# Two sequences by turns: the order of token groups in a fused linear-attention and two-layer feed-forward kernel

## The chip, the cores and the metric

The kernel runs on one core of one Trainium2 chip. The core has a tensor engine (PE, with its weight loads as PEld), a vector engine (DVE), a scalar engine (ACT), GpSimd (POOL), and a sync engine (SP) that here issues nearly all transfers. The metric is device time in microseconds (us) of one execution; lower is better. A difference of about 2% is what a measurement of this kernel can surely tell from no change.

## What is computed

A linear attention with a decay per head and dimension gives x; a sum of four experts, weighted per token, follows, and then a feed-forward layer with a sigmoid gate. Sizes: 2 sequences of 768 tokens, 8 heads of 48, so 1536 tokens of width 384; 4 experts of 1024 hidden units; a last layer of 2048.

```python
for t in range(S):                      # per sequence and head
    cur = einsum('bhd,bhe->bhde', u[None] * kt, vt)
    y[:, :, t] = einsum('bhd,bhde->bhe', rt, state + cur)
    state = w[None, :, :, None] * state + einsum('bhd,bhe->bhde', kt, vt)
...
p = domain_probs / (domain_probs.sum(-1, keepdims=True) + 1e-09)
for e in range(E):
    h = np.maximum(x @ w1[e], 0.0)
    out += p[:, e:e + 1] * (h @ w2[e])
...
h = x @ w_in
g = h * (1.0 / (1.0 + np.exp(-1.702 * h)))
return g @ w_out
```

## The kernel before

The attention works on 12 groups of 128 tokens, `G`; groups 0 to 5 are the first sequence, 6 to 11 the second. For each group (`attention`) r and k are scaled by powers of the decay (`rr` on DVE, `kk` on DVE for groups 0 and 1 and on POOL for the others, `kb` on ACT), PE forms the scores of the 8 heads in two halves (`sc`), DVE copies them under the causal mask into `at` (whose diagonal, r u k of a token itself, POOL has made from `ruk` and `ss`), and PE multiplies `at` with the values (`y`). A group that isn't the first of its sequence adds the product of `rr` with the state `sn` to `y`. The state of the next group comes from `kc` (k by a table `tab`, on POOL), the product `kv` (PE), its part within the heads `sn` (DVE), and the decayed state before, `tn` (POOL). `y` is split into two float32r parts, `xh` (ACT) and `xl` (DVE).

The feed-forward layers run in six blocks of eight chunks of 128 hidden units: four experts, and the last layer in two halves. A unit is one chunk with one tile of tokens, 256 tokens in block 0 and 512 in the others. Its weights are split into `wh` (ACT) and `wl` (DVE), its hidden values into `gh` (ACT) and `gl` (DVE); each product is three matmuls (high by high, low by high, high by low), nine for `up` and nine for `dn`. The first tile of block 0, tokens 0 to 255, needs groups 0 and 1 alone. The router weights `pb` of an expert, 1536 floats, are copied to all 128 partitions through a scratch `pscr` in HBM. At the end DVE adds two blocks (`final`, into `tp`) and SP stores `tp` to `out_t`.

Nothing is issued in the order of the code. A planner (`Plan`) takes every operation with its engine, an assumed cost, a due time and what it reads and writes, plays them through and writes out one order for each engine; an engine then executes its own list strictly in that order. Changed due times or dependences can so move any operation of the early part. Matmuls called `warm`, on data of no meaning, fill planned gaps of PE before the first unit. Near the start there is also a check of the range of the decays, `wr`, `mm` and `flag`: six small DVE instructions that nothing but the end of the program needs.

Of the kernel before, what the change touches and what calls it, by code (L numbers as in the profile page):

```python
# [18 lines left out]
P = 128  # L19
# [17 lines left out]
NB = 8                  # chunks on chip, split  # L37
# [9 lines left out]
class Plan:  # L47
    """Operations in an order that is right one after another, and the order in which they are issued.

    Each names the engine, what it takes of it, when it is wanted, what it reads, writes and which  # L50
    buffers it takes. An engine that is free takes, of the operations that could start, the one wanted
    first.
    """
# [70 lines left out]
# what a transfer or an operation adds before another engine can go on  # L124
# [15 lines left out]
def c_mm(m, n, wide=True):  # L140
    # a product in float32, or in two parts
    return 2 * max(m / 1200, n / 1200) if wide else max(m / 1200, n / 2400)


def narrowing(nc, hi, lo, a, m, r):
    """The steps from the two words of a float64 to the float32 nearest to it."""
    dve, pool = nc.vector, nc.gpsimd
    f = lambda t: t().bitcast(F32)
    return (
        lambda: dve.tensor_scalar(out=m(), in0=hi(), scalar1=0x7fffffff, scalar2=None, op0=ALU.bitwise_and),  # L150
        lambda: dve.tensor_scalar(out=f(m), in0=f(m), scalar1=HI_MIN, scalar2=2.0 ** 16, op0=ALU.max, op1=ALU.mult),  # L151
        lambda: dve.tensor_scalar(  # L152
            out=m(), in0=m(), scalar1=4, scalar2=1, op0=ALU.logical_shift_left, op1=ALU.logical_shift_right),
        lambda: dve.scalar_tensor_tensor(  # L154
            out=a(), in0=hi(), scalar=-0x80000000, in1=m(), op0=ALU.bitwise_and, op1=ALU.bitwise_or),
        lambda: dve.tensor_scalar(out=m(), in0=a(), scalar1=-0x800000, scalar2=None, op0=ALU.bitwise_and),  # L156
        lambda: dve.scalar_tensor_tensor(  # L157
            out=f(m), in0=lo().bitcast(U32), scalar=2.0 ** -52, in1=f(m), op0=ALU.mult, op1=ALU.mult),
        lambda: pool.tensor_tensor(out=r(), in0=f(a), in1=f(m), op=ALU.add),  # L159
    )  # L160


def times(a, n, m):
    # the columns of a, m times
    return a.rearrange("p (o i) -> p o i", o=1).to_broadcast([n, m, a.shape[-1]])
# [18 lines left out]
def general(ctx: ExitStack, tc: tile.TileContext, wv, cst, msk, pscr, rk, tok, wts, wts2, out):  # L184
    """The whole again, for any decay: no power of it is negative.

    Within a group, the second half of a block of tokens looks at its first half, for blocks of every size.
    """
# [152 lines left out]
def body(outer: ExitStack, tc: tile.TileContext, wv, cst, msk, dp, rk, tok, wts, wts2, out):  # L341
# [45 lines left out]
    def warm():  # L387
        # keeps the tensor engine's clock up while its operands are on their way
        if "warm" not in T:
            T["warm"] = ps_dn.tile([P, 512], F32, tag="dn0", name="warm")  # L390
        pe.matmul(T["warm"][:, :G], lhsT=acc[:, 0, :G], rhs=acc[:, 0, :G], start=True, stop=True)
# [10 lines left out]
    def load_group(g, dues):  # L402
        def one(i):
            if i == 0:
                T["rk", g] = rk_p.tile([PD, 2, NP, G], F32, tag="rk", name="rk")
                sp.dma_start(T["rk", g], rk[g])
            elif i == 1:
                T["tok", g] = rk_p.tile([P, 2, DM], F32, tag="tok", name="tok")
                sp.dma_start(T["tok", g], tok[g, :, 0:2])
            else:  # L410
                T["val", g] = rk_p.tile([P, 2, DM], F32, tag="val", name="val")
                sp.dma_start(T["val", g], tok[g, :, 2:4])
# [72 lines left out]
    def power_table():  # L485
        # kept finite where the general path takes over
# [14 lines left out]
    def tables(due):  # L501
        # for the state: w^(191-j) by token, w^128 within the blocks of the heads
        kt = ac_p.tile([PD, NP, G], F32, name="kt")
# [54 lines left out]
    def load_p(e, due):  # L558
        def fn():
            T["pb", e] = pb_p.tile([P, NT], F32, tag="pb", name="pb")  # L560
            sp.dma_start(
                T["pb", e], pscr[e].rearrange("p n -> (p n)").rearrange("(a n) -> a n", a=1).to_broadcast([P, NT]))
        add("dma", 2.2, due, fn, reads=["pscr"], writes=[("pb", e)], takes=[("pb", 1, ("pb", e))])

# [1 line left out]
    def attention(g, due):  # L566
        first, final = g % GPB == 0, g % GPB == GPB - 1
# [7 lines left out]
        # decayed r and k, by dimension  # L575
# [28 lines left out]
        # r u k of a token itself, on the diagonal  # L604
# [66 lines left out]
        # the state: the sum of k v, decayed  # L671
        if not final:
# [13 lines left out]
            def own_():  # L686
                new(("sn", g + 1), [PD, NP, PD])
                dve.tensor_tensor(out=T["sn", g + 1], in0=T[kv], in1=times(own, PD, NP), op=ALU.mult)
# [3 lines left out]
            add("dve", c_dve(DM), due["kv"] + 1, own_, reads=[kv, "cs1"], writes=[("sn", g + 1)],  # L692
                takes=[("sn", 2, ("sn", g + 1))])
            if not first:
                add("pool", c_pool(DM), due["kv"] + 2, lambda: pool.tensor_tensor(
                    out=T["sn", g + 1], in0=T["sn", g + 1], in1=T["tn", g], op=ALU.add),
                    reads=[("tn", g)], writes=[("sn", g + 1)])
            if g % GPB < GPB - 2:
                def decay():
                    new(("tn", g + 1), [PD, NP, PD], bufs=1)  # L700
                    pool.tensor_tensor(out=T["tn", g + 1], in0=T["sn", g + 1], in1=wg, op=ALU.mult)
                add("pool", c_pool(DM), due["kv"] + 6, decay, reads=[("sn", g + 1), "wg"], writes=[("tn", g + 1)],
                    takes=[("tn", 1, ("tn", g + 1))])
# [59 lines left out]
    def unit(i):  # L763
# [68 lines left out]
        for j in range(3):  # L832
            # the last of all goes out in two parts
# [10 lines left out]
    def end(blk, j, dn, t0, n, due, cols):  # L844
# [27 lines left out]
        if blk == 0:  # L872
            add("dve", c_dve(n), due, scaled, reads=[dn, ("pb", 0), "warm"], writes=AK)
# [11 lines left out]
        else:  # L885
# [4 lines left out]
            o = out[j * P:(j + 1) * P, t0 + cols.start:t0 + cols.stop]  # L890
            add("dma", n / 640, due, lambda: sp.dma_start(o, T[TP][:, cols]), reads=[part])

# [1 line left out]
    def dues(b, d, prep):  # L894
# [10 lines left out]
    tables(-925)  # L905
    attention(0, {"scale": -970, "bonus": -970, "sc": (-960, -950), "mask": (-959, -949), "kc": -890, "kv": -880,
                  "av": (-955, -945), "out": -940})
    attention(1, {"scale": -930, "bonus": -930, "sc": (-920, -910), "mask": (-919, -909), "kc": -700, "kv": -600,
                  "av": (-860, -850), "out": -840})
# [100 lines left out]
```

## Time and profile before

| what | value |
|---|---|
| median of 3 runs | 710.98 us |
| the three runs | 706.25, 710.98 and 2824.54 us |
| span of the profiled execution | 704.3 us |
| PE busy, share of the span | 96% |
| DVE, ACT and POOL busy | 53%, 28% and 24% |
| mean granted clock of PE | 0.997 of full |

The times list no separate own time of the profiled execution: beside its span of 704.3 us stands the fastest run, 706.25 us. Busy shares are averages over stages that have different limits; in the first 40 us PE waits for other engines, and between 410 and 530 us for DVE.

### The profile page before, as it was taken

What the parts mean: (1) busy time and instruction counts of PE and PEld (TensorE: products, weight loads), DVE (VectorE), ACT (ScalarE), POOL (GpSimd) and SP (SyncE); (2) the same over time, 40 slices, a digit from 0 to 9 for tenths busy, and PEclk for the clock granted to TensorE, in tenths of its full rate; (3) what the DMA queues carried; (4) which work ended last, traced back from release to release, by engine and by line L of the source; (5) the groups of instructions that cost most, each with busy time, mean ns of one, the idle gap of its engine ahead of it and who ended that gap; (6) DMA issues with size and microseconds to landing.
All of it is one profiled execution on the core that took longest, in us unless ns stands there. A gap on an engine that the chain in (4) does not pass through costs nothing.

```text
span 704.3 us, 8976 instructions
## 1 busy us (share of the span) xinstructions
PE 677.8 (96%) x3644; PEld 580.4 (82%) x3644; DVE 374.9 (53%) x559; ACT 194.7 (28%) x351; POOL 169.2 (24%) x139
## 2 busy tenths in 40 slices
PE   8799999999999999999999998899799999999996
PEld 7799999999988888888888766688478888888885
DVE  7895544543622134412136999859993345434333
ACT  3432222212421123211123112133323344432231
POOL 6999356500001020202020334133430000000000
PEclk9999999999999999999999999999999999999999
DMA  7985223100420002300003442402100000001011
GB/s 228 288 241 168 66 68 91 46 1 1 136 89 1 0 1 91 129 5 0 1 24 111 180 134 91 134 1 89 46 0 1 1 0 1 0 1 46 1 45 49
DMA packets 12546, 45.90 MB, mean 65 GB/s; under 512 B 2129, under 2 KB 2642, under 8 KB 12498
## 3 DMA queue, kind: packets, MB, share of 16 engines
q1 hardware_dynamic: 12498, 45.26, 19.9%
q8 instruction: 30, 0.49, 0.3%
q14 instruction: 18, 0.15, 0.1%
HBM read 42.87 MB, written 2.38 MB: 64 GB/s over the span
## 4 chain that ended last, share of the span: by engine, by line
PE 76%; DVE 17%; POOL 3%; issue 2%; DMA 1%; ACT 0%; SPq 0%; DVEq 0%; POOLq 0%
PE dn L829 34%; PE up L775 34%; PE sc L661 4%; PE y L714 3%; DVE m L150 2%; DVE a L154 2%; DVE m L151 2%; DVE gl L794 1%; DVE wl L479 1%; DVE m L152 1%; PE y L718 1%; DVE m L156 1%; DVE m L157 1%; DMA rk<-in_rk 1%; DVE tp L855 1%
## 5 line engine op out<-in xcount | busy, mean ns | idle before, releaser
L775 PE MATMUL up<-xh,wh 128*128 128x512 f32 (+1 forms) x504 | 185.6, 368 | 8.2 <-DVE gl L794 6.6
L829 PE MATMUL dn<-gh,wh 128*128 128x512 f32 (+1 forms) x512 | 182.9, 357 | 4.3 <-DVE tp L855 4.1
L829 PE MATMUL dn<-gl,wh 128*128 128x512 f32 (+1 forms) x512 | 182.6, 357 | 2.4 <-DVE gl L813 2.4
L829 PE MATMUL dn<-gh,wl 128*128 128x512 f32 (+1 forms) x512 | 182.2, 356 | 0.0
L775 PE MATMUL up<-xl,wh 128*128 128x512 f32 (+1 forms) x504 | 181.0, 359 | 0.5 <-DVE xl L738 0.5
L775 PE MATMUL up<-xh,wl 128*128 128x512 f32 (+1 forms) x504 | 180.8, 359 | 0.0
L794 DVE SCALAR_TENSOR_TENSOR gl<-up,gh 128x512 fp32r<-128x512 f32 (+1 forms) x120 | 69.7, 582 | 168.0 <-ACT gh L788 167.7
L788 ACT ACTIVATE gh<-up 128x512 fp32r<-128x512 f32 (+1 forms) x120 | 61.4, 512 | 306.1 <-PE up L775 305.9
L775 PEld LDWEIGHTS up<-xh,wh 128*128 128x128 f32 x504 | 95.1, 189 | 26.2 <-DVE gl L794 10.4
L829 PEld LDWEIGHTS dn<-gh,wh 128*128 128x128 f32 x512 | 96.6, 189 | 20.8 <-DVE tp L855 2.3
L829 PEld LDWEIGHTS dn<-gl,wh 128*128 128x128 f32 x512 | 96.7, 189 | 17.1 <-DVE gl L813 3.0
L829 PEld LDWEIGHTS dn<-gh,wl 128*128 128x128 f32 x512 | 96.6, 189 | 13.7
L775 PEld LDWEIGHTS up<-xh,wl 128*128 128x128 f32 x504 | 95.0, 188 | 14.2
L775 PEld LDWEIGHTS up<-xl,wh 128*128 128x128 f32 x504 | 95.1, 189 | 13.9 <-DVE xl L738 0.7
L858 POOL TENSOR_TENSOR acc<-acc,tp 128x512 f32<-128x512 f32 x27 | 37.8, 1409 | 219.1 <-DVE tp L855 218.7
L809 DVE TENSOR_TENSOR gf<-up,sg 128x512 f32<-128x512 f32 x48 | 33.1, 690 | 75.2 <-ACT sg L805 75.2
L159 POOL TENSOR_TENSOR r<-a,m 128x768 f32<-128x768 f32 x16 | 32.0, 2001 | 90.8 <-DVE m L157 85.5
L805 ACT ACTIVATE sg<-up 128x512 f32<-128x512 f32 x48 | 28.6, 596 | 82.4 <-PE up L775 82.0
L813 DVE TENSOR_TENSOR gl<-gf,gh 128x512 fp32r<-128x512 f32 x48 | 33.4, 696 | 22.6 <-ACT gh L788 21.7
L788 ACT ACTIVATE gh<-gf 128x512 fp32r<-128x512 f32 x48 | 30.4, 632 | 41.4 <-DVE gf L809 41.0
L479 DVE TENSOR_TENSOR wl<-w,wh 128x768 fp32r<-128x768 f32 x32 | 34.1, 1069 | 2.8 <-ACT wh L475 2.2
L714 PE MATMUL y<-at,val 128*96 128x128 f32 x192 | 29.5, 281 | 1.6 <-DVE at L664 1.6
(78 smaller groups left out, 544.9 us busy)
## 6 DMA issues: line engine op xcount, KB each, us to landing
w<-in_wts SPq DMA_DIRECT2D x32, 768.0 KB, 4.5
rk<-in_rk SPq DMA_DIRECT2D x12, 384.0 KB, 4.4
tok<-in_tok SPq DMA_DIRECT2D x12, 384.0 KB, 4.5
val<-in_tok SPq DMA_DIRECT2D x12, 384.0 KB, 3.7
pb<-pscr SPq DMA_DIRECT2D x4, 768.0 KB, 4.5
out_t<-tp SPq DMA_DIRECT2D x8, 256.0 KB, 2.0
out_t<-tp SPq DMA_DIRECT2D x2, 128.0 KB, 3.4
cs<-in_cst SPq DMA_DIRECT2D x1, 192.5 KB, 4.3
```

What stands on the lines that cost most here:

```text
L159: lambda: pool.tensor_tensor(out=r(), in0=f(a), in1=f(m), op=ALU.add),
L479: dve.tensor_tensor(out=T[L_], in0=src(), in1=T[H_].bitcast(F32), op=ALU.subtract)
L661: pe.matmul(sc[:, j, :], lhsT=a[:n, h // 2, :], rhs=T[RR][:n, h // 2, :], start=True, stop=True)
L714: pe.matmul(y[:, p, :], lhsT=v2[:, h].rearrange("p b d -> p (b d)"), rhs=T["at", g, half][:, h % NP, :], start=hh == 0, stop=first and hh ...
L775: pe.matmul(T[U][:, :n], lhsT=a[:, s], rhs=b, start=d + k == 0, stop=d + k == 4)
L788: act.activation(out=T[GH][:, :n], in_=T[src][:, :n], func=f)
L794: dve.scalar_tensor_tensor(out=T[GL][:, :n], in0=T[U][:, :n], scalar=0.0, in1=T[GH][:, :n].bitcast(F32), op0=ALU.max, op1=ALU.subtract)
L805: act.activation(out=T[SG][:, :n], in_=T[U][:, :n], func=ACTF.Sigmoid, scale=1.702)
L809: dve.tensor_tensor(out=T[GF][:, :n], in0=T[U][:, :n], in1=T[SG][:, :n], op=ALU.mult)
L813: dve.tensor_tensor(out=T[GL][:, :n], in0=T[GF][:, :n], in1=T[GH][:, :n].bitcast(F32), op=ALU.subtract)
L829: pe.matmul(T[dn][:, cols], lhsT=T[a][:, s], rhs=T[b][:, cols], start=first and k == 0, stop=last and k == 2)
L858: pool.tensor_tensor(out=av, in0=av, in1=T[TP][:, :n], op=ALU.add)
```

## The change

The groups of the two sequences are taken by turns: with `ORDER`, place q of the plan holds group q // 2 of sequence q % 2. Places 0 and 1 are then both first groups, places 10 and 11 both final ones, and a state is handed on from place g to place g + 2; so three `sn` buffers are kept instead of two. The decay `tn` of a state is now made at the group that uses it. As the columns of x, of `acc` and of the output tiles now stand by turns too, `pb` is loaded and `out_t` is stored in two transfers each, with runs of 128 tokens (512 bytes), the second store being issued by ACT. The decay table `kt` is put into room of `acc` that is not yet in use. Due times of the tables, of `kc`, `kv`, and of group 1's `av` and `out` are changed.

```diff
+ORDER = [q % B * GPB + q // B for q in range(NG)]
...
-                sp.dma_start(T["rk", g], rk[g])
+                sp.dma_start(T["rk", g], rk[ORDER[g]])
...
-        kt = ac_p.tile([PD, NP, G], F32, name="kt")
+        kt = acc[:PD, 2, :NP * G].rearrange("p (a i) -> p a i", a=NP)
...
-            sp.dma_start(
-                T["pb", e], pscr[e].rearrange("p n -> (p n)").rearrange("(a n) -> a n", a=1).to_broadcast([P, NT]))
+            for b in range(B):
+                sp.dma_start(
+                    T["pb", e].rearrange("p (g b i) -> p b g i", b=B, i=G)[:, b],
+                    pscr[e].rearrange("p n -> (p n)").rearrange("(a b g i) -> b a g i", a=1, b=B, i=G)[b].to_broadcast(
+                        [P, GPB, G]))
...
-        first, final = g % GPB == 0, g % GPB == GPB - 1
+
+        first, final = g < B, g >= NG - B
...
-                new(("sn", g + 1), [PD, NP, PD])
-                dve.tensor_tensor(out=T["sn", g + 1], in0=T[kv], in1=times(own, PD, NP), op=ALU.mult)
+                new(("sn", g + B), [PD, NP, PD], bufs=3)
+                dve.tensor_tensor(out=T["sn", g + B], in0=T[kv], in1=times(own, PD, NP), op=ALU.mult)
...
             if not first:
+                def decay():
+                    new(("tn", g), [PD, NP, PD], bufs=1)
+                    pool.tensor_tensor(out=T["tn", g], in0=T["sn", g], in1=wg, op=ALU.mult)
+                add("pool", c_pool(DM), due["kc"], decay, reads=[("sn", g), "wg"], writes=[("tn", g)],
+                    takes=[("tn", 1, ("tn", g))])
...
-            add("dve", c_dve(n), due, scaled, reads=[dn, ("pb", 0), "warm"], writes=AK)
+            add("dve", c_dve(n), due, scaled, reads=[dn, ("pb", 0), "warm", "tab"], writes=AK)
...
-            add("dma", n / 640, due, lambda: sp.dma_start(o, T[TP][:, cols]), reads=[part])
...
+            def store():
+                for b in range(B):
+                    (act if b else sp).dma_start(
+                        o[:, b], T[TP][:, cols].rearrange("p (g b i) -> p b g i", b=B, i=G)[:, b])
+            add("dma", n / 640, due, store, reads=[part])
...
-    tables(-925)
-    attention(0, {"scale": -970, "bonus": -970, "sc": (-960, -950), "mask": (-959, -949), "kc": -890, "kv": -880,
+    tables(-870)
+    attention(0, {"scale": -970, "bonus": -970, "sc": (-960, -950), "mask": (-959, -949), "kc": -790, "kv": -780,
                   "av": (-955, -945), "out": -940})
     attention(1, {"scale": -930, "bonus": -930, "sc": (-920, -910), "mask": (-919, -909), "kc": -700, "kv": -600,
-                  "av": (-860, -850), "out": -840})
+                  "av": (-915, -905), "out": -900})
```

The lists below show what the planner writes out, for three engines; a number behind a name is the buffer's, and a row with x4 stands for that many instructions.

On PE, from the scores of group 1 to the first unit, the list before is this (`y_297` is group 1, `kv_274` and `kv_326` are the products of groups 0 and 1 for the state):

```order
L661 MATMUL sc_260<-rr_201,kb_203 128x128 x2
L684 MATMUL kv_274<-val_147,kc_240 96x96 x4
L391 MATMUL warm_120<-acc_96 128x128 x5
L714 MATMUL y_297<-at_252,val_197 96x128 x2
L718 MATMUL y_297<-rr_201,sn_287 96x128
...
L684 MATMUL kv_326<-val_197,kc_293 96x96 x4
L661 MATMUL sc_336<-rr_295,kk_279 128x128 x2
L661 MATMUL sc_336<-rr_295,kb_306 128x128 x2
L775 MATMUL up_350<-xh_97,wh_289 128x256
```

and now it is this (`y_276` is group 1):

```order
L667 MATMUL sc_245<-rr_200,kb_202 128x128 x2
L513 MATMUL tab_ps_259<-cs_100,acc_96 128x96 x4
L393 MATMUL warm_119<-acc_96 128x128 x3
L719 MATMUL y_276<-at_243,val_196 96x128 x4
L719 MATMUL y_276<-at_255,val_196 96x128 x4
L690 MATMUL kv_302<-val_146,kc_287 96x96 x4
L667 MATMUL sc_311<-rr_281,kk_269 128x128 x2
L667 MATMUL sc_311<-rr_281,kb_299 128x128 x2
L393 MATMUL warm_119<-acc_96 128x128 x6
L690 MATMUL kv_344<-val_196,kc_325 96x96 x4
L393 MATMUL warm_119<-acc_96 128x128 x2
L780 MATMUL up_358<-xh_97,wh_283 128x256
```

Group 1 no longer reads a state, and `kv` of group 0 has moved behind its `y`; the products with a state that left here stand at place 6 now, which before was a first group.

On DVE, from the masks of group 1 on, the list before is this (`rr_295` is group 2, `rr_332` group 3; the `xl` rows are group 1, the `wl` rows chunks 0 to 2):

```order
L664 COPY_PREDICATED at_267<-cs_100,sc_260 128x512
L688 TENSOR_TENSOR sn_287<-kv_274,cs_100 96x384
L595 TENSOR_TENSOR rr_295<-rk_214,rp_104 96x512
L479 TENSOR_TENSOR wl_308<-w_229,wh_289 128x768
L479 TENSOR_TENSOR wl_320<-w_229,wh_310 128x768
L595 TENSOR_TENSOR rr_332<-rk_270,rp_104 96x512
L735 TENSOR_TENSOR xl_98<-y_297,xh_97 96x3x128
L738 TENSOR_TENSOR xl_98<-y_297,xh_97 32x128 x3
L688 TENSOR_TENSOR sn_355<-kv_326,cs_100 96x384
L622 TENSOR_REDUCE ss_365<-ruk_322 128x8
L479 TENSOR_TENSOR wl_384<-w_304,wh_367 128x768
```

and now it is this:

```order
L670 COPY_PREDICATED at_255<-cs_100,sc_245 128x512
L601 TENSOR_TENSOR rr_281<-rk_213,rp_104 96x512
L528 TENSOR_TENSOR wr_113<-wr_113 1x384
L529 TENSOR_REDUCE mm_114<-wr_113 1x1
...
L533 TENSOR_TENSOR flag_108<-mm_114 1x1
L694 TENSOR_TENSOR sn_319<-kv_302,cs_100 96x384
L740 TENSOR_TENSOR xl_98<-y_276,xh_97 96x3x128
L743 TENSOR_TENSOR xl_98<-y_276,xh_97 32x128 x3
L481 TENSOR_TENSOR wl_342<-w_228,wh_283 128x768
L694 TENSOR_TENSOR sn_353<-kv_344,cs_100 96x384
L481 TENSOR_TENSOR wl_362<-w_228,wh_307 128x768
L601 TENSOR_TENSOR rr_376<-rk_257,rp_104 96x512
```

The check of the decays (`wr` to `flag`), which stood behind group 2's masks, has come ahead of group 1's `xl`, and the first two `wl` have gone behind it.

On ACT, in the last block where the first tile of the output is stored, the list before is this (`sg` and `gh` of two successive units):

```order
L788 ACTIVATE gh_5209<-gf_5204 128x512
L805 ACTIVATE sg_5230<-up_5200 128x512
L788 ACTIVATE gh_5245<-gf_5237 128x512
L805 ACTIVATE sg_5264<-up_5233 128x512
L788 ACTIVATE gh_5275<-gf_5270 128x512
```

and now it is this:

```order
L793 ACTIVATE gh_5218<-gf_5213 128x512
L900 DMA out_t<-tp_5228 128x2x128
L810 ACTIVATE sg_5240<-up_5209 128x512
L900 DMA out_t<-tp_5233 128x2x128
L793 ACTIVATE gh_5256<-gf_5248 128x512
L900 DMA out_t<-tp_5254 128x2x128
L810 ACTIVATE sg_5276<-up_5244 128x512
```

Three stores, each of which waits for DVE's `tp`, stand between activations now; it is so again at the second tile, and four stores stand behind the last activation.

## Rows read from the trace of the kernel before

**Rows 1.** The page: span, and busy time of each engine.

```profile
span 704.3 us, 8976 instructions
PE 677.8 (96%) x3644; PEld 580.4 (82%) x3644; DVE 374.9 (53%) x559; ACT 194.7 (28%) x351; POOL 169.2 (24%) x139
```

**Rows 2.** Stretches: length; PE, PEld, DVE, ACT, POOL busy (instructions); clock, DMA share, GB/s.

```profile
10.00:20.00 10.00, 8.37 (x65) 7.35 (x66) 8.26 (x16) 4.30 (x10) 9.68 (x12) 1.00 0.82 248
25.00:33.00 8.00, 4.64 (x34) 4.24 (x35) 6.28 (x11) 3.72 (x7) 7.86 (x7) 1.00 0.99 283
33.00:38.00 5.00, 5.00 (x31) 4.88 (x31) 4.05 (x9) 1.11 (x2) 4.58 (x5) 0.66 0.43 104
38.00:50.00 12.00, 12.00 (x104) 11.49 (x103) 10.84 (x18) 4.60 (x10) 11.63 (x8) 1.00 0.90 276
```

**Rows 3.** Timeline of PE, 15 to 50 us: start, us, instruction, idle before.

```profile
20.26 0.24 PEld L718 LDWEIGHTS y<-rr,sn 96*96 96x96 f32 x2 [0.15 <-DVE sn L688]
25.49 0.28 PE L775 MATMUL up<-xh,wl 128*128 128x256 f32 x1
...
27.28 0.28 PE L775 MATMUL up<-xh,wl 128*128 128x256 f32 x1
29.00 0.39 PE L775 MATMUL up<-xh,wh 128*128 128x256 f32 x1 [1.45 <-DVE gl L794]
32.71 0.71 PE L661 MATMUL sc<-rr,kk 48*128 48x128 f32 x4 [1.65 <-DVE at L664]
40.44 0.36 PE L775 MATMUL up<-xh,wh 128*128 128x256 f32 x1
...
45.75 0.84 PE L684 MATMUL kv<-val,kc 128*96 128x96 f32 x8
```

**Rows 4.** Timeline of DVE and POOL, 18 to 40 us.

```profile
18.42 1.36 DVE L664 COPY_PREDICATED at<-cs,sc 128x512 f32<-128x512 int32 x2
20.13 0.86 DVE L595 TENSOR_TENSOR rr<-rk,rp 96x512 f32<-96x512 f32 x1
24.93 0.92 DVE L738 TENSOR_TENSOR xl<-y,xh 32x128 fp32r<-32x128 f32 x3 [0.33 <-ACT xh L731]
29.26 1.73 DVE L479 TENSOR_TENSOR wl<-w,wh 128x768 fp32r<-128x768 f32 x1 [0.31 <-ACT wh L475]
30.05 2.83 POOL L638 TENSOR_TENSOR at<-ss,cs 128x512 f32<-128x512 f32 x2
34.80 0.53 DVE L526 TENSOR_TENSOR wr<-wr 1x384 f32<-1x384 f32 x1
37.60 0.53 DVE L622 TENSOR_REDUCE ss<-ruk 128x8 f32<-128x384 f32 x1
38.06 0.94 DVE L479 TENSOR_TENSOR wl<-w,wh 128x768 fp32r<-128x768 f32 x1
```

**Rows 5.** Transfers: KB each, median us to landing; issues and first use of `pb`.

```profile
pscr<-pn SPq DMA_DIRECT2D x1, 24.0 KB, 2.6
wvs<-in_wv SPq DMA_DIRECT2D x1, 1.5 KB, 1.8
L852 DVE TENSOR_TENSOR acc<-dn,pb x18: 416/424/425, 62.2 to 194.0; 128x256 f32<-128x256 f32 x18
L561 SPq DMA_DIRECT2D pb<-pscr x4: 326/327/382, 40.5 to 393.3; - x4
DMA to landing us min/median/max: 4.1/4.5/7.8
```

**Rows 6.** Timeline of ACT, DVE and SP where a tile is stored, and at the end.

```profile
636.27 0.60 ACT L805 ACTIVATE sg<-up 128x512 f32<-128x512 f32 x1 [2.09 <-PE up L775]
...
634.82 1.40 DVE L870 TENSOR_TENSOR tp<-dn,acc 128x512 f32<-128x512 f32 x2
...
698.16 0.78 DVE L870 TENSOR_TENSOR tp<-dn,acc 128x256 f32<-128x256 f32 x2 [0.38 <-PE dn L829]
697.13 2.31 SPq L891 DMA_DIRECT2D out_t<-tp  x4
```

More of the change, by code (lines that the diff above doesn't have):

```diff
@@ L405, in one @@
                 T["rk", g] = rk_p.tile([PD, 2, NP, G], F32, tag="rk", name="rk")
-                sp.dma_start(T["rk", g], rk[g])
+                sp.dma_start(T["rk", g], rk[ORDER[g]])
             elif i == 1:
                 T["tok", g] = rk_p.tile([P, 2, DM], F32, tag="tok", name="tok")
-                sp.dma_start(T["tok", g], tok[g, :, 0:2])
+                sp.dma_start(T["tok", g], tok[ORDER[g], :, 0:2])
             else:
                 T["val", g] = rk_p.tile([P, 2, DM], F32, tag="val", name="val")
-                sp.dma_start(T["val", g], tok[g, :, 2:4])
+                sp.dma_start(T["val", g], tok[ORDER[g], :, 2:4])
         for i, k in enumerate(("rk", "tok", "val")):
@@ L686, in own_ @@
             def own_():
-                new(("sn", g + 1), [PD, NP, PD])
-                dve.tensor_tensor(out=T["sn", g + 1], in0=T[kv], in1=times(own, PD, NP), op=ALU.mult)
+                new(("sn", g + B), [PD, NP, PD], bufs=3)
+                dve.tensor_tensor(out=T["sn", g + B], in0=T[kv], in1=times(own, PD, NP), op=ALU.mult)
             add("pool", c_pool(DM), due["kc"], by_token, reads=[tk_, "tab"], writes=[KC], takes=[("kc", 1, KC)])
             add("pe", 4 * c_mm(PD, PD), due["kv"], products, reads=[KC, vl_], writes=[kv], takes=[("kv", 1, kv)])
-            add("dve", c_dve(DM), due["kv"] + 1, own_, reads=[kv, "cs1"], writes=[("sn", g + 1)],
-                takes=[("sn", 2, ("sn", g + 1))])
+            add("dve", c_dve(DM), due["kv"] + 1, own_, reads=[kv, "cs1"], writes=[("sn", g + B)],
+                takes=[("sn", 3, ("sn", g + B))])
             if not first:
-                add("pool", c_pool(DM), due["kv"] + 2, lambda: pool.tensor_tensor(
[L696 to L703, printed above, removed]
+                def decay():
[3 more added lines that the diff above has]
+                    takes=[("tn", 1, ("tn", g))])
+                add("pool", c_pool(DM), due["kv"] + 2, lambda: pool.tensor_tensor(
+                    out=T["sn", g + B], in0=T["sn", g + B], in1=T["tn", g], op=ALU.add),
+                    reads=[("tn", g)], writes=[("sn", g + B)])
         for half in range(2):
@@ L889, in end @@
                 takes=[("tp", 3, TP)] if cols.start == 0 else ())
-            o = out[j * P:(j + 1) * P, t0 + cols.start:t0 + cols.stop]
-            add("dma", n / 640, due, lambda: sp.dma_start(o, T[TP][:, cols]), reads=[part])
+            g0 = (t0 + cols.start) // G // B
+            o = out[j * P:(j + 1) * P].rearrange("p (b g i) -> p b g i", b=B, i=G)[:, :, g0:g0 + n // G // B]
+            def store():
[3 more added lines that the diff above has]
+            add("dma", n / 640, due, store, reads=[part])
     def dues(b, d, prep):
```

## The prediction

> **What bounds the kernel now.** I read the page first: PE is busy for 677.8 of 704.3 us, so only 26.5 us are idle anywhere, and the share of the other engines is far lower [rows 1]. A change that leaves PE its work can win at most idle time, time at a lower clock, and what lies behind the last matmul. Next I read the stretches of the first 50 us, because the lists differ there: between 25 and 33 us PE is busy for 4.64 of 8.00 us, and in the 5 us after that its clock stands at 0.66 on average, which means that part of them ran at 1.2 instead of 2.4 GHz; from 38 us on PE is busy without a gap [rows 2]. So the start has three losses. Then the timeline of PE gives their causes: 1.45 us until `gl` of the first unit, 1.65 us until a mask of group 2, and a first low-weight matmul at 25.49 us that came as soon as DVE was done with group 1's `xl` [rows 3, 4]. What limits PE there is the order of DVE's and POOL's lists. Later stalls (PE waits for DVE around the conversion of the last layer's weights) stay: from about place 700 of PE's list on the two lists agree up to the output, and so do DVE's.
>
> **The state, removed from group 1.** The reader should first see how little this wait cost: the weights of the first product with a state came 0.15 us late because of `sn` [rows 3]. The products themselves aren't saved. Forty stand in PE's list before and forty now, because place 6, a first group before, now has a state. The same holds for `kv`, `sn` and `tn`. So PE's total is the same, and the direct gain is 0.15 us. All that matters is what the planner did with the freedom.
>
> **The new order at the start.** I walk DVE's new list from the end of group 1's two masks, 18.42 + 1.36 = 19.78 us, up to which nothing has left DVE's list [rows 4]. Then come `rr` (0.86), the check of the decays, which in the trace ran from 34.80 to 37.60, so 2.80 us, a `sn` (taken as the equally wide `ss`, 0.53), and group 1's `xl` (0.53 for the wide and 0.92 for the three narrow instructions): 25.42 us. Before, it ended at 24.93 + 0.92 = 25.85 us [rows 4]. What group 1 wins without a state is eaten by the check that stands ahead. And now the first `wl` comes behind `xl`, 0.94 us: the first low-weight matmul can start at 26.36 us, not at 25.49. The first unit is 0.9 us late.
>
> After that the new list is better. It goes on with `sn`, `wl`, `rr` (0.53 + 0.94 + 0.86, 28.69 us), `gl` (0.42, from the 128 x 256 row in [rows 5]; 29.11), `wl`, `gl`, `ss` (31.0), `wl`, `gl` (32.36). The next is group 2's mask, for which POOL needs `ss` and half of 2.83 us [rows 4], 32.4 us, and the mask takes 0.68: 33.1 us. For some 17 handovers and for the slower ones among the `wl` (one took 1.73 us, [rows 4]) I add 0.4, so group 2's second scores start at 33.5 us, against 32.71 before [rows 3]: 0.8 us later. But PE has by then done more. By the new list it has also behind it `kv` of group 2 (0.84 us), the last three `dn` of unit 0, and nine matmuls of units 3 and 1; a matmul of this width starts every (27.28 - 25.49) / 15 = 0.12 us [rows 3], so that is 0.84 + 12 x 0.12 = 2.3 us. Net 1.5 us are won without any help from the clock.
>
> **The clock.** The 5 us from 33 on had a mean of 0.66, so 5 x 0.34 = 1.7 us of full-speed work was lost, after 8 us in which PE was busy for 58% (4.64 of 8.00); between 10 and 20 us it was busy for 84% and the clock stayed at 1.00 [rows 2]. In the new order PE's work between 25.4 and 33.5 us is 36 matmuls for units 0 to 2, `kv`, and the nine: 45 x 0.12 + 0.84 = 6.2 of 8.1 us, 77%. That lies nearer to 84 than to 58, and the gaps are shorter (the longest, ahead of the first `wl`, about 0.9 us against 1.65). I take the clock to hold, so that the start wins 1.5 + 1.7 = 3.2 us; if it falls as before, it wins 1.5.
>
> **The queues.** The 24 KB for `pscr` and the two `pb` now go ahead of group 3's `tok` and `val` on SP's queue, and SP waits there until `pscr` has landed, 2.6 us [rows 5]. Behind it stand those and the fourth `w`. The second and the third `w` go earlier than before, and the fourth waits for `wl` in both; its chunks are needed by DVE only some ten us later, which hides it. If that cover failed, a late `w` would cost its landing beyond the need, at most about 2 us. `pb` had 62.2 - 40.5 = 21.7 us from issue to use, against landings of 4.1 to 7.8 [rows 5]; twice the packets don't reach that. `kt` inside `acc` adds a wait of the first `acc` writes for `tab`, which is made 40 us earlier: nothing. Three `sn` buffers cost room alone.
>
> **The output.** Stores on ACT wait for DVE, and behind the first waits the next `sg`. DVE's first two `tp` end at 634.82 + 1.40 = 636.22; the second half of that is needed only by the second store, the first is done at about 635.5, and an issue, which this trace shows on SP alone, takes 0.33 us [rows 5, 6]. `sg` started at 636.27, behind 2.09 us of idle time [rows 6]. So ACT's three issues fit, and the same holds at the second tile; if they didn't, PE still works two units ahead. At the end SP's four issues took 2.31 us, paced by `tp`, not by SP, and the last `tp` ended at 698.94 [rows 6], so a second queue wins nothing there. Runs of 512 bytes: the last tile goes out in 3 x 128 x 4 = 1,536 of them, against 2 x 128 of 2 KB and 2 x 128 of 1 KB before, 1,024 more. Their price isn't in the trace. Nearest are 512 runs of 48 bytes (`pscr`, 2.6 us) and 96 of 16 bytes (`wvs`, 1.8): 0.8 us for 416 runs, 1.9 ns each [rows 5], or 2.0 us for 1,024; from below, halves that run side by side could win 0.5 us. Runs ten times as long hide most of such a price behind their own bytes, so I take 0.4 us, and keep 2.0 and -0.5 for the range. The Trainium skill (DMA: Bandwidth & Descriptors, section Specifications) puts the least size for full rate at 512 bytes; by it this term would be 0 and the sum 0.4 us lower. No run so far shows 512-byte runs.
>
> **The sum** is -3.2 + 0.4 = -2.8 us, a span of 701.5 us. Two of the runs shown agree, 706.25 and 710.98 us, and the third is four times as long; the span is 2.0 us below the faster. I take 707.4 as the time before, between the faster one and the mean of the two (708.6), so the forecast is 704.6 us. The median shown is 3.6 us above that base.
>
> **Rivals.** (a) *Nothing won*: the clock falls as before and DVE drifts by another us or so, as `wl` at 1.73 us shows it can while POOL works; -1.5 + 0.4 + 1.1 = 0, 707.4 us. For it speaks that DVE's list is hardly shorter than the time it has. (b) *Slower*: the waits of PE for `wl`, `gl` and the mask between 25 and 33 us bring the clock down earlier than before, and it stays at 1.2 GHz through the units that follow. Ten such us lose 5 us of work, 3.3 more than the 1.7 of now; with the order's 1.5 on the other side, 0.4 for the output and 1 us of DVE's drift this gives +3.2, 710.6 us. It decides once the low stretch lasts for over 2 x (1.7 + 1.5) = 6.4 us. Against it: 77% is more than 58%. (c) *More won*: PE's gaps of 1.45 and 1.65 us vanish whole, and so does the loss of clock: 4.8 us, from the base 702.6 us; it needs DVE faster than its rows. (d) *The output's runs* cost their upper bound, 2.0 us: 707.4 - 3.2 + 2.0 = 706.2 us. That the change doesn't do what it says is excluded, for the list shows group 1 without a state; that this was worth little is in the forecast.
>
> **How the numbers follow.** The forecast has 0.5, (a) 0.2, (b) 0.12, (c) 0.1, (d) 0.08. Range: from (c) on the faster run, 706.25 - 4.8 = 701.4, to (b), 710.6, and a little more on both sides for the run-to-run difference of the two runs (4.7 us): 700 to 712. Two per cent, which is about what a measurement of this kernel can tell from no change, is 14 us, more than half of all of PE's idle time: faster by that 0.03, slower 0.03 (a stage that no row here points to), within it 0.94.
>
> **What would show it.** Right: the first low-weight matmul at 26 to 27 us, `up` of unit 3 ahead of group 2's second scores, a clock of 1.00 from 25 to 45 us, the last `tp` 2.5 to 3.5 us earlier, PE's busy time down by about 2 us. Wrong: a stretch at 1.2 GHz; PE waits over 1 us between 26 and 34 us; a wait of ACT for a store ahead of `sg` with PE idle behind it; over 6 us from the last `tp` to the end (5.4 now).

## The result, and the profile after

The changed kernel takes 716.89 us (median of 4 runs, 715.01 to 718.13), against 710.15 for the kernel before (median of 4 runs): ratio 1.0101, 95% interval 1.0074 to 1.0128. One of those four runs took 2824.54 us, and the ratio leaves it out. The forecast was 704.6 us and the range 700 to 712. The profiled execution took 717.11 us with a span of 715.3 us, 11.0 us more than the span from which the prediction was made. It is slower, by half of the two per cent that count as a difference.

The page of the changed kernel, its first two rows and the row of PE's clock in 40 slices:

```profile
span 715.3 us, 9023 instructions
PE 685.5 (96%) x3656; PEld 586.7 (82%) x3656; DVE 376.0 (53%) x559; ACT 194.3 (27%) x351; POOL 166.2 (23%) x139
...
PEclk8997999999999999999999999999999999999999
```

PE is busy 7.7 us longer than in [rows 1], with the same products: its matmuls ran at a lower clock somewhere. The clock's row says where: most of all the first slice and the fourth (54 to 72 us). So I looked at stretches there (length; PE, PEld, DVE, ACT, POOL busy; clock, DMA share, GB/s), the first four being those of [rows 2], the last two from the stage where PE waits for DVE:

```profile
10.00:20.00 10.00, 9.66 (x50) 8.71 (x50) 6.30 (x12) 2.84 (x9) 8.32 (x10) 0.66 0.83 283
25.00:33.00 8.00, 6.62 (x54) 6.00 (x53) 7.84 (x14) 2.92 (x5) 5.61 (x5) 1.00 0.87 248
33.00:38.00 5.00, 4.85 (x42) 4.53 (x41) 4.27 (x8) 1.85 (x3) 3.83 (x3) 1.00 1.00 362
38.00:50.00 12.00, 11.34 (x95) 10.55 (x93) 9.43 (x15) 4.15 (x9) 11.84 (x10) 1.00 0.86 262
54.00:56.00 2.00, 0.78 (x7) 0.57 (x5) 2.00 (x2) 0.00 (x0) 2.00 (x3) 1.00 1.00 332
56.00:58.00 2.00, 0.00 (x0) 0.00 (x0) 1.61 (x6) 1.53 (x4) 1.92 (x3) 1.00 0.78 300
58.00:68.00 10.00, 9.99 (x43) 9.09 (x44) 2.64 (x5) 1.10 (x2) 3.56 (x4) 0.53 0.15 43
68.00:70.00 2.00, 2.00 (x17) 2.00 (x17) 0.23 (x1) 0.39 (x1) 0.69 (x1) 0.81 0.00 0
...
510.00:515.00 5.00, 3.13 (x8) 2.29 (x9) 5.00 (x8) 2.48 (x4) 2.22 (x2) 0.75 0.07 30
515.00:520.00 5.00, 4.51 (x18) 3.32 (x18) 5.00 (x7) 2.27 (x4) 2.26 (x2) 0.91 0.00 0
```

Two things stand out. From 10 to 20 us the clock stands at 0.66 (1.00 in [rows 2]). And at 56 to 58 us PE does nothing at all, after which it works for ten us at 0.53, nearly all of it at 1.2 GHz: 43 matmuls where a full-speed stretch of that length held some 87. The stretches on which the prediction had looked, 25 to 50 us, run at 1.00 without an exception. A smaller loss lies late: 5 x 0.25 + 5 x 0.09 = 1.7 us of work between 510 and 520 us, where the profile of the kernel before has 1.00.

The timeline of PE over both places (start, us, instruction, idle before and its releaser):

```profile
28.75 0.39 PE L780 MATMUL up<-xh,wl 128*128 128x256 f32 x1 [0.50 <-DVE wl L481]
...
32.18 0.39 PE L834 MATMUL dn<-gl,wh 128*128 128x256 f32 x1 [0.53 <-DVE gl L799]
...
36.41 0.71 PE L667 MATMUL sc<-rr,kk 48*128 48x128 f32 x4 [0.15 <-DVE at L670]
...
58.01 0.39 PE L780 MATMUL up<-xh,wh 128*128 128x256 f32 x1 [3.23 <-DVE gl L799]
```

The two long waits of [rows 3] (1.45 and 1.65 us) have gone, as hoped: none between 25 and 37 us is over 0.53. In their place stands one of 3.23 us, for `gl`. What was in front of `gl`? The timeline of DVE:

```profile
51.36 0.55 DVE L628 TENSOR_REDUCE ss<-ruk 128x8 f32<-128x384 f32 x1 [1.20 <-POOL ruk L622]
51.94 3.87 DVE L601 TENSOR_TENSOR rr<-rk,rp 96x512 f32<-96x512 f32 x1
55.73 0.54 DVE L740 TENSOR_TENSOR xl<-y,xh 96x384 fp32r<-96x384 f32 x1
56.61 0.89 DVE L743 TENSOR_TENSOR xl<-y,xh 32x128 fp32r<-32x128 f32 x3 [0.33 <-ACT xh L736]
57.53 0.76 DVE L799 SCALAR_TENSOR_TENSOR gl<-up,gh 128x256 fp32r<-128x256 f32 x2
```

and that of POOL beside it:

```profile
51.29 1.00 POOL L683 TENSOR_TENSOR kc<-tok,tab 128x384 f32<-128x384 f32 x1
52.26 2.04 POOL L644 TENSOR_TENSOR at<-ss,cs 128x512 f32<-128x512 f32 x2
54.27 0.99 POOL L703 TENSOR_TENSOR tn<-sn,wg 96x384 f32<-96x384 f32 x1
55.23 1.71 POOL L591 TENSOR_TENSOR kk<-rk,kp 96x512 f32<-96x512 f32 x1
```

One `rr`, that of place 5, takes 3.87 us, where [rows 4] have one of 0.86. It ends at 55.81, which is 0.55 us after POOL's row of four instructions without a gap ends (54.27 + 0.99 = 55.26); and POOL's `kk`, which comes just then, takes 1.71 us where another takes 1.26. Behind `rr` wait `xl` and the two `gl` that PE needs, and PE had run out of other work at 54.8. Nobody needs this `rr` soon: the scores of place 5 come behind those of place 4, which start at 59.2.

At the end, DVE's last `tp`, and the stores on SP's and ACT's queues:

```profile
708.52 0.78 DVE L875 TENSOR_TENSOR tp<-dn,acc 128x256 f32<-128x256 f32 x2 [0.38 <-PE dn L834]
...
707.48 2.32 SPq L900 DMA_DIRECT2D out_t<-tp  x4
707.49 2.36 ACTq L900 DMA_DIRECT2D out_t<-tp  x4
```

From the last `tp` (709.30) to the end are 6.00 us, against 704.3 - 698.94 = 5.36 before [rows 1, 6].

### The profile page after: what moved, and what is told of

Read it like the earlier page. It is cut to its first block, busy times and chain, and to the rows that moved or that the text cites. A ratio compares the mean times of both kernels' runs of the same rounds, so it can differ in the third digit from the quotient of the medians.

```text
span 715.3 us, 9023 instructions
## 1 busy us (share of the span) xinstructions
PE 685.5 (96%) x3656; PEld 586.7 (82%) x3656; DVE 376.0 (53%) x559; ACT 194.3 (27%) x351; POOL 166.2 (23%) x139
## 4 chain that ended last, share of the span: by engine, by line
PE 74%; DVE 18%; issue 2%; POOL 2%; DMA 2%; ACT 0%; SPq 0%; DVEq 0%; POOLq 0%
PE dn L834 33%; PE up L780 33%; PE sc L667 4%; PE y L719 3%; DVE m L152 2%; DVE a L156 2%; DVE m L153 2%; DVE wl L481 1%; DVE gl L799 1%; DVE m L154 1%; DVE rr L601 1%; PE y L723 1%; DMA w<-in_wts 1%; DVE m L158 1%; DVE m L159 1%
## 5 line engine op out<-in xcount | busy, mean ns | idle before, releaser
L780 PEld LDWEIGHTS up<-xh,wh 128*128 128x128 f32 x504 | 95.9, 190 | 29.3 <-DVE gl L799 13.7
L780 PEld LDWEIGHTS up<-xl,wh 128*128 128x128 f32 x504 | 95.8, 190 | 13.2
```

The lines of the kernel that those rows point to most:

```text
L780: pe.matmul(T[U][:, :n], lhsT=a[:, s], rhs=b, start=d + k == 0, stop=d + k == 4)
```

## The experiments

Three theories. **1**: the loss is made between 52 and 70 us, by the slow `rr` ahead of `gl` and by the low clock behind PE's wait. **2**: it is the low clock of 10 to 20 us. **3**: it is the transfers in two pieces. The kernel before, measured beside them on the same chip, took 709.18 us (25 runs) beside e1 to e4, 707.83 (15 runs) beside e5 to e8 and 708.72 (17 runs) beside e9 to e12; ratios are against those.

**e1, `rr` behind `xl`.** A dependency that the planner sees, and no more:

```diff
-            add("dve", c_dve(n), d + 1, r_, reads=[rk_, *tabr], writes=[RR], takes=[("rr", 2, RR)] if i == 0 else ())
+            add("dve", c_dve(n), d + 1, r_, reads=[rk_, *tabr, *([("xl", g - 1, 3)] if g == 5 else [])], writes=[RR], takes=[("rr", 2, RR)] if i == 0 else ())
```

> One rr (that of the sixth group, at 51.94 us in the changed kernel) goes behind the xl of the group before it; the lists of PE and ACT stay as they are. Theory 1 (the loss is made at 52 to 58 us: rr takes 3.87 us beside POOL, xl and two gl stand behind it, PE runs dry for 3.23 us, and its clock is low for the 11 us after that): the 3.23 us go, and with them some 5.2 us of low clock; 717.1 - 8.4 = 708.7 us, 706.5 to 711. Theory 2 (the low clock of 10 to 18 us is what counts, and PE would be late for DVE anyway): another wait takes its place, 715 to 718. Theory 3 (the transfers in two pieces cost it): no change, 715 to 718.

711.05 us (10 runs), ratio 1.0025 (1.0011 to 1.0040): three quarters of the 1.01% have gone. PE's first low-weight matmul, its wait at the place in question, the new wait that comes later, and two stretches:

```profile
29.43 0.39 PE L780 MATMUL up<-xh,wl 128*128 128x256 f32 x1 [0.50 <-DVE wl L481]
...
56.03 0.38 PE L780 MATMUL up<-xh,wh 128*128 128x256 f32 x1 [0.53 <-DVE gl L799]
...
72.38 0.68 PE L667 MATMUL sc<-rr,kk 48*128 48x128 f32 x4 [0.90 <-DVE rr L601]
```

```profile
10.00:20.00 10.00, 7.93 (x44) 7.13 (x42) 5.45 (x9) 2.41 (x8) 8.09 (x11) 0.66 1.02 277
...
58.00:68.00 10.00, 10.00 (x87) 9.75 (x86) 4.88 (x10) 1.88 (x4) 8.01 (x9) 1.00 0.10 24
```

The wait is 0.53 us and the ten us behind it hold 87 matmuls at 1.00 instead of 43. The clock from 10 to 20 us is as low as in the changed kernel, so theory 2 has no part in this. The gain is 5.8 us, not 8.4, and the time lies just past the range given. The wait shrank by 2.7 us and the clock gave back some 4.7 (10 x 0.47). Against that, the first unit came 0.7 us later in this execution (29.43 against 28.75), and the scores of place 5 now wait 0.90 us, at 72.38, for the `rr` that was moved: 2.7 + 4.7 - 0.7 - 0.9 = 5.8.

**e5, POOL held back.** The first experiment shows that `rr` was in the way, not why it was slow. Here it stays where it was; POOL waits instead (the planner is told so by the key of that `xl` in the reads of the diagonals, `tn`, `kk` and `ruk` that follow; PE's list stays the same, and the others change only behind this place):

```diff
                     new(at, [P, NP, G])
+                    if g == 4 and half == 0:
+                        z = at_p.tile([P, 1], F32, name="z")
+                        pool.tensor_copy(z[PD:P], xl[PD:P, 2, 4 * G - 1:4 * G].bitcast(F32))
                     pool.tensor_tensor(
```

> The changed kernel with rr left where it is, ahead of xl and gl; POOL is held back instead: its two diagonals of the fifth group now wait (behind a copy of one column, 32 x 1) until DVE has written the xl of the fourth, so that POOL reads nothing while rr runs. Theory 1 with its cause (rr takes 3.87 us because POOL's at x2 and tn run without a gap beside it, and its 0.68 us begin only when they end): rr takes 0.7 to 1.4 us, PE is idle for under 1.2 us ahead of gl, the clock stays at 1.00 from 58 to 69 us, 710 us (708 to 712). Rival (rr waits for its operand rk, or DVE is slow there for another reason): rr still takes over 3 us, 716 to 718.

710.85 us (4 runs), ratio 1.0044 (1.0027 to 1.0060). DVE's `rr`, POOL before and behind it, and PE's wait:

```profile
52.46 0.91 DVE L601 TENSOR_TENSOR rr<-rk,rp 96x512 f32<-96x512 f32 x1
...
51.82 1.00 POOL L686 TENSOR_TENSOR kc<-tok,tab 128x384 f32<-128x384 f32 x1
55.45 0.18 POOL L646 COPY z<-xl 32x1 f32<-32x1 f32 x1 [2.64 <-DVE xl L746]
...
55.82 0.39 PE L783 MATMUL up<-xh,wh 128*128 128x256 f32 x1 [0.53 <-DVE gl L802]
```

The same `rr` with the same operands takes 0.91 us instead of 3.87, and again ends 0.55 us after the POOL instruction beside it (52.82 to 53.37). The rival, a late operand, falls. So the cause is shown: POOL's instructions beside it make `rr` slow. Why they do, no run here shows. The Trainium skill (SBUF — State Buffer, section Who interferes with whom) says that a DVE instruction with two SBUF inputs contends with a GpSimd instruction that reads SBUF, and calls the port pair that they share an exclusive lock; by that rule `rr` and `wl`, with two SBUF inputs, are exposed, and `xl` and `gl` of these groups, with one input in PSUM, are not. The rows of the changed kernel agree: `xl` and `gl` take 0.54 and 0.38 us each beside a busy POOL.

**e2, longer warm-up.** Six of the 19 warm-up calls ahead of the first scores issue twice (a call is two matmuls in the trace):

```diff
+        T["nw"] = T.get("nw", 0) + 1
+        for _ in range(2 if 13 < T["nw"] <= 19 else 1):
-        pe.matmul(T["warm"][:, :G], lhsT=acc[:, 0, :G], rhs=acc[:, 0, :G], start=True, stop=True)
+            pe.matmul(T["warm"][:, :G], lhsT=acc[:, 0, :G], rhs=acc[:, 0, :G], start=True, stop=True)
```

> The changed kernel with 50 instead of 38 warm-up matmuls ahead of the first scores, all else in the same order. Theory 2: PE stays busy until some 8.2 us, the clock stays at 1.00 from 10 to 18 us, the first low-weight matmul comes at 26.4 instead of 28.75 us, and 2.3 us are won, 714.8 us (713.5 to 716); with them the later stall might shrink, not vanish. Theory 1: the clock of the start is worth at most those 2.3 us, since PE waits for DVE at 55 us in any case; 714.5 to 717. Against both: the clock falls at 10 us all the same, 717.

714.71 us (4 runs), ratio 1.0075 (1.0048 to 1.0101). The number lies in the ranges of theories 1 and 2 alike, so it decides nothing; the mechanism of theory 2 didn't show: the clock still fell (0.83 from 10 to 20 us), and the first low-weight matmul came at 28.04, 0.7 us earlier, not 2.3. PE's wait of 3.22 us for `gl` is there, with 43 matmuls from 58 to 68 us at 0.50. The last `acc` of block 0 is 0.8 us earlier than in the changed kernel (202.3 against 203.1), the last `tp` 2.0. The other 1.2 us lie behind it: from 205 us on PE's waits for DVE add up to 12.0 us here, to 13.2 in the changed kernel.

**e3, old due times.** Groups by turns, with the planner's table of before:

```diff
-    tables(-870)
-    attention(0, {"scale": -970, "bonus": -970, "sc": (-960, -950), "mask": (-959, -949), "kc": -790, "kv": -780,
+    tables(-925)
+    attention(0, {"scale": -970, "bonus": -970, "sc": (-960, -950), "mask": (-959, -949), "kc": -890, "kv": -880,
...
-                  "av": (-915, -905), "out": -900})
+                  "av": (-860, -850), "out": -840})
```

> The changed kernel with the due times of the kernel before (tables, kc and kv of the first group, values and out of the second). Groups still go by turns. Theory 1 (turns set the order of DVE from 40 us on, due times only the first 30 us): rr still stands ahead of the xl and gl that PE waits for, 713 to 718. Rival (the new due times make the loss, since they pull the check of the decays ahead of the second xl): near the kernel before, 706 to 711.

710.36 us (10 runs, 708.00 to 715.29), ratio 1.0028 (1.0002 to 1.0053). Theory 1 gave 713 to 718 and missed; the rival's range holds the number, but its reason, the check of the decays, isn't borne out by e6 below. Theory 1 was too narrow here. The slow `rr` is there, the one of place 5 too, but PE had more work in store: from its start on 4.3 us of it, against 2.8 in the changed kernel:

```profile
49.05 3.73 DVE L601 TENSOR_TENSOR rr<-rk,rp 96x512 f32<-96x512 f32 x1 [0.20 <-PE y L723]
52.70 0.54 DVE L740 TENSOR_TENSOR xl<-y,xh 96x384 fp32r<-96x384 f32 x1
...
49.21 2.05 POOL L644 TENSOR_TENSOR at<-ss,cs 128x512 f32<-128x512 f32 x2
51.22 1.01 POOL L703 TENSOR_TENSOR tn<-sn,wg 96x384 f32<-96x384 f32 x1
...
54.98 0.39 PE L780 MATMUL up<-xh,wh 128*128 128x256 f32 x1 [1.66 <-DVE gl L799]
```

PE waited 1.66 us here (and 1.87 at another `rr` of 2.89 us), and the clock stayed at 1.00 behind both. By the medians, then, the turns with the two pieces cost a quarter of the loss (by the interval, anything from nothing to half), and the rest came with the new due times, which shift what stands beside what. The profile is that of one of the faster runs (708.44): five of the ten took 708.0 to 709.8 us at a mean clock of 0.992 to 0.995, five 710.9 to 715.3 at 0.980 to 0.986, and of those none has a profile.

**e4, e11, e12: two pieces in the kernel before.** Router weights and outputs as in the changed kernel, order of the groups as before:

```diff
-            add("dma", n / 640, due, lambda: sp.dma_start(o, T[TP][:, cols]), reads=[part])
+            def store():
+                for b in range(B):
+                    (act if b else sp).dma_start(
+                        o.rearrange("p (g b i) -> p b g i", b=B, i=G)[:, b],
+                        T[TP][:, cols].rearrange("p (g b i) -> p b g i", b=B, i=G)[:, b])
+            add("dma", n / 640, due, store, reads=[part])
```

> The kernel before, its order of groups unchanged, with its router weights and its outputs moved in two transfers of 512-byte runs, the second store on ACT's queue. Theory 3 (this part costs the time): 3 to 10 us over the kernel before. Theories 1 and 2: only the end counts, 0 to 1 us over it (the term of the prediction was 0.4).

710.74 us (10 runs), ratio 1.0019 (0.9995 to 1.0044): 1.6 us over the median of the kernel before, more than the 0 to 1 of theories 1 and 2, but not clear of no change and well under the 3 of theory 3, which falls as the main cause. From the last `tp` to the end it takes 6.14 us. Two more kernels ask what makes the end longer. One puts both stores on SP (`sp.dma_start` in place of `(act if b else sp).dma_start`):

> The fourth experiment's kernel with both stores of a tile on SP's queue. The end only: if the 512-byte runs make the end longer, the time from the last tp to the end of the span stays at 6.0 to 6.2 us, or grows since SP issues eight stores; if ACT's queue does it, it goes back to 5.4.

The other cuts each store into halves of neighbouring columns:

```diff
+                h = n // 2
+                for b in range(2):
+                    (act if b else sp).dma_start(
+                        o[:, b * h:(b + 1) * h], T[TP][:, cols.start + b * h:cols.start + (b + 1) * h])
```

> The kernel before with each store cut into two halves of neighbouring columns (runs of 1 KB, the last two of 512 bytes), the second on ACT's queue; router weights as before. If the 512-byte runs make the end longer: 5.4 to 5.9 us from the last tp to the end; if ACT's queue does it: 6.0 to 6.2.

The stores on SP's queue in the first of them, and on both queues in the second:

```profile
700.39 5.55 SPq L897 DMA_DIRECT2D out_t<-tp  x8
```

```profile
701.01 2.31 SPq L895 DMA_DIRECT2D out_t<-tp  x4
701.02 2.35 ACTq L895 DMA_DIRECT2D out_t<-tp  x4
```

With all eight on SP the issues alone take 5.55 us, and the end 8.6 (710.8 - 702.20). With halves on two queues it is 6.4 (709.2 - 702.83), so the longer end comes without the turn-wise layout too, once a store is cut in two. ACT's queue is the cheaper place for the second. What costs the 0.6 to 1.0 us stays open. The 512-byte runs alone don't explain it: the last stores land 3.3 us after their issue where all are on SP's queue, against 3.4 in the kernel before (with twice the bytes in each), and after 3.7 to 4.0 us where two queues store at once. (One run each: 712.53 and 711.01 us.)

**e10, the kernel before, again**, unchanged:

> The kernel before, unchanged, once more, for its clock in the first 30 us. If the profile from which the prediction was made was an exception: the clock is low somewhere between 10 and 26 us, as in the fourth experiment, whose lists are the same there, and the time is 708 to 712 us. If the clock of the start is a property of this order: 1.00 up to 33 us, as in that profile, and 706 us.

709.04 us, span 707.2. Two stretches of it:

```profile
10.00:20.00 10.00, 8.20 (x53) 7.20 (x53) 6.50 (x13) 3.99 (x10) 8.93 (x12) 0.83 0.82 221
...
45.00:52.00 7.00, 5.57 (x40) 5.36 (x38) 4.32 (x7) 0.38 (x1) 6.57 (x6) 0.76 0.70 238
```

So the low clock of the start doesn't need the change: of the thirteen other profiles here all have it low somewhere between 10 and 26 us, and only the one behind the prediction has 1.00. That profile was a rare one. Its mean clock over the whole span is 0.997; of the 57 runs of this kernel beside the experiments four have that, and they took 706.04 to 706.38 us. The 37 at 0.991 to 0.994 took 707.3 to 710.7, and the 16 at 0.985 to 0.989 took 710.1 to 712.3. The second stretch shows the kernel before losing time to the same neighbours, the other way round: POOL's `kc` at 44.99 takes 2.36 us beside an `rr` and a `wl`, PE waits 1.43 us for it, and its clock falls.

**e6, e7, e9, e8: looking for a better version.** The first, e6, adds to `rr` behind `xl` the longer warm-up and a late check of the decays:

```diff
-        add("dve", 1.8, due + 6, check, reads=["wr"], writes=["flag"])
+        add("dve", 1.8, due + 6, check, reads=["wr", ("xl", 7, 3)], writes=["flag"])
```

> The changed kernel with three edits: rr of the sixth group behind xl, as in the first experiment; 50 warm-up matmuls; the check of the decays (2.6 us of DVE ahead of the second xl) moved behind the xl of the eighth group. If the losses add up: 711.05 - 2.2 for the warm-up - 1 to 2.5 for the check = 707 us (706 to 709), under the kernel before. If PE at the start waits for POOL's diagonals and not for DVE's list: the check gives nothing, 709 us or more.

710.11 us (6 runs), ratio 1.0031 (1.0010 to 1.0052): the losses don't add up, the check and the warm-up give nothing on top. The second, e7, starts from the old due times:

> Groups by turns with the due times of the kernel before, and the three edits: every rr from the fifth group on behind the xl ahead of it, the check late, 50 warm-up matmuls. Theory 1: the two waits of PE for gl behind a slow rr (1.87 and 1.66 us in the third experiment) go, 710.4 - 3.5 = 707 us, and 706 with the check away (705 to 708.5). Rival (rr behind xl makes the scores of the next group late): 710 to 713.

719.75 us (4 runs), ratio 1.0170 (1.0153 to 1.0187), far off both expectations; part of why is told below. The third, e9, holds POOL back at two places of the old-due-times kernel (places 3 and 4, behind the `rr` of the next place):

> The third experiment's kernel (groups by turns, due times of the kernel before) with POOL held back at two places: its diagonals of the fourth and of the fifth group wait, behind a copy of one column (96 x 1), for the rr that follows on DVE; the lists are otherwise the same. Theory 1: the two rr (2.89 and 3.73 us there) take 0.7 to 1.4, PE's waits of 1.87 and 1.66 us for gl shrink by some 2.5 us, 710.4 - 2.5 = 707.9 us (706.5 to 709.5), which would be level with the kernel before or just under it. Rival (POOL's work, 1.5 and 0.7 us later, makes the masks or kc late instead): 710 to 712.

713.51 us (12 runs, 705.56 to 716.20), ratio 1.0033 (1.0002 to 1.0064). The held places did as expected (those two `rr` took 0.69 and 0.67 us), though PE then waited 2.18 us for a `kc`, as the rival had it. But a third `rr`, of place 3, which had taken 1.24 us in the third experiment, met POOL's row in this run. DVE, POOL and PE there:

```profile
30.13 4.40 DVE L609 TENSOR_TENSOR rr<-rk,rp 96x512 f32<-96x512 f32 x1
34.45 0.41 DVE L810 SCALAR_TENSOR_TENSOR gl<-up,gh 128x256 fp32r<-128x256 f32 x1
...
30.98 2.05 POOL L655 TENSOR_TENSOR at<-ss,cs 128x512 f32<-128x512 f32 x2
32.98 1.00 POOL L626 TENSOR_TENSOR ruk<-tok 128x384 f32<-128x384 f32 x1
...
34.92 0.39 PE L845 MATMUL dn<-gl,wh 128*128 128x256 f32 x1 [2.77 <-DVE gl L810]
```

and the stretch that followed:

```profile
36.00:42.00 6.00, 6.00 (x27) 5.43 (x26) 3.91 (x7) 0.84 (x1) 1.35 (x1) 0.50 1.04 336
```

Again `rr` ends 0.55 us behind POOL's row (33.98 to 34.53), PE waits 2.77 us for the `gl` behind it, and the clock falls to 0.50. In e7 the same `rr` took 4.47 us, with the same 2.77 us of PE's; there PE was also idle for 2.69 us between 100 and 150 us, where e1 to e5 have none: its scores waited 0.9 us each time for an `rr` behind `xl`, as the rival had it. This `rr` started at 26.44 us in e3, at 27.35 in e7 and at 30.13 in e9. So a delay at the start, which differs from run to run with the clock there, may decide which `rr` meets POOL's row. That would explain why e9's runs lie far apart, 705.56 us at a mean clock of 0.992 and 713.4 to 714.9 at 0.980 to 0.984, but only one of them has a profile, so it isn't shown.

Last, e8, the kernel before with the late check and the longer warm-up:

> The kernel before with the late check and 50 warm-up matmuls: no turns, no pieces. If the loss at the start is one of clock and of DVE's list whatever the order of the groups: 709.2 - 2 to 3.5 = 706.5 us (705 to 708), as good as groups by turns with the same edits or better. If the state's wait is what keeps the start of the kernel before slow: no gain, 708.5 to 710.

707.59 us (10 runs), ratio 0.9992 (0.9973 to 1.0012): no gain. (The time lies in the range of the first theory only because the kernel before took 707.83 beside it, not 709.2.) No version here beats the kernel before.

## Why the prediction was wrong

- **The state's wait is worth little**: right. It was 0.15 us, and nothing that followed hung on it.
- **The walk of DVE's list**: right in its total, in part by luck. From the end of group 1's masks to the first low-weight matmul it gave 26.36 - 19.78 = 6.6 us, and 28.75 - 22.12 = 6.6 were measured; to group 2's second scores 13.7, measured 14.3. But the terms missed both ways: the check took 2.0 us instead of 2.80 (in the profile before, its last instruction had taken 1.09 us, here 0.25), `rr` 1.41 instead of 0.86 and `wl` 1.43 instead of 0.94. And the row it is compared with was misread: the last `xl` of the profile before ended at 25.85 us, behind the low-weight matmul at 25.49. Both waits over a microsecond vanished as said, and the clock was 1.00 from 25 to 45 us.
- **Its start**: wrong by 2.3 us. The end of the masks, "up to which nothing has left DVE's list", was taken over at 19.78 us from the profile before, where the clock was at 1.00 from 10 to 20 us. Here it was 0.66, `y` of group 0 took 3.48 us, and the masks of group 1 ended at 20.76 + 1.36 = 22.12. That is no effect of the change (the kernel before has it too), but it belongs in the base: 707.4 leaned on a lucky execution, and the medians of this kernel beside the experiments are 707.8 to 709.2. Of the 3.2 us that the new order was to win at the start, some 0.9 can be found (2.3 less the 1.4 in the last point below).
- **Where it stopped**: this is the step that failed. The walk ended at 33.5 us, the lists were said to agree from "about place 700", which PE reaches only at about 98 us, and what lies between was put at nothing. At 52 us the new list has `rr` ahead of `xl` and two `gl`. With `rr` at the 0.86 us that I used, the `gl` would have come three us earlier and PE would hardly have waited; with `rr` moved away, the first experiment left 0.53. At 3.87 us it cost 3.23 us of waiting and, by the ten us at 0.53 behind it, some 5 us of clock. The walk has 0.86 for every `rr`; rows of the same trace had it at 1.4 to 2.9 us while POOL worked, and I took the one value that stood in the walk.
- **"I take the clock to hold"**: right for the stretch it was said of, wrong for the kernel. Rival (b) named the mechanism (ten us at 1.2 GHz) and the price of 5 us; it put it at 25 to 33 us and had no wait of three us ahead of it, so its 710.6 stayed 6 us short. The comparison of busy shares (77% nearer to 84 than to 58) was no ground for it: from 10 to 20 us the kernel before, run again with the same list, was busy for 82% and had 0.83. Nor does the length of a wait decide alone: behind 1.43 us in that run the clock fell, behind 1.87 us in e3 it stayed.
- **The signs**: the clock of 1.00 from 25 to 45 us came and was no sign of success; the wait of over 1 us was looked for between 26 and 34 us only and came at 54.8; the stretch at 1.2 GHz was the one sign that spoke.
- **The queues hid what they should**: right. No wait of PE for a transfer shows.
- **The output**: 0.64 us instead of 0.4, a term of the right size for a reason that isn't shown: I costed it by the 512-byte runs, no run here prices them alone, and with all stores on SP's queue they landed no later than before.
- **The sum** as it was: of the 1.01%, the slow `rr` and the clock behind it 0.6 to 0.8 (two experiments), the end 0.1, the rest, 0.15 to 0.35, not placed. The two profiles can be set side by side more closely, by DVE's last `acc` of block 0, which [rows 5] have at 194.0:

```profile
L857 DVE TENSOR_TENSOR acc<-dn,pb x18: 417/425/425, 71.1 to 203.1; 128x256 f32<-128x256 f32 x18
```

Of the 11.0 us between the spans, 9.1 are there by then: 3.2 for the wait, less 0.65 for one that the kernel before has at 72 us, some 5.1 for the clock from 56 to 70 us, and the 1.4 left over lie ahead of it, where the start came 2.3 us late. Another 1.3 us come between 203 us and the last `tp`, with the low clock from 510 to 520 us, and 0.6 at the end. That late stretch comes and goes: e2 and e5 have one, e1 and e3 don't, and e4, e11 and e12 have one with the old order of groups, so it doesn't need the turns.

## What to carry to other kernels

A list that a planner writes with fixed costs (0.60 us for this `rr`) is only as good as the slowest that an instruction gets beside its neighbours: look for products of two SBUF tiles on DVE while POOL runs a row without gaps, and see what is queued behind them. Walk a changed order to the point where the lists agree again, not to where the old waits were. And before a saving of half a per cent is costed from one profile, find out whether that execution is a typical one.

## What was not expected of the hardware

An `rr` of 0.68 us doesn't always get in between two of POOL's instructions: it waited out up to four in a row, and in six profiles (3.87, 3.85, 3.73, 4.47, 4.40 and 0.91 us) it ended 0.54 to 0.55 us after the last of them. At other places it got in after the first, though POOL's next stood right behind, and then that one took longer, as `ruk` here in the changed kernel (1.46 us, 1.0 elsewhere):

```profile
40.43 1.64 DVE L601 TENSOR_TENSOR rr<-rk,rp 96x512 f32<-96x512 f32 x1 [0.99 <-PE y L723]
...
40.26 1.26 POOL L591 TENSOR_TENSOR kk<-rk,kp 96x512 f32<-96x512 f32 x1
41.49 1.46 POOL L618 TENSOR_TENSOR ruk<-tok 128x384 f32<-128x384 f32 x1
```

What decides how many it waits for isn't shown. And the granted clock in the first 26 us differs from one execution to the next with the same list: 1.00 throughout in one profile of the kernel before, and 0.83 from 10 to 20 us in the other, in which the 38 warm-up matmuls took 6.87 us instead of 7.28.
